# A new program order for all engines of a windowed attention and two mixture layers, with the first key loads in another sequence

## Chip, cores and metric

The kernel runs on one core of a Trainium2 chip. The metric is the device time of one execution in microseconds (us); lower is better. A core has five engines that run their own instruction lists: TensorE (PE, matrix products), VectorE (DVE), ScalarE (ACT), GpSimd (POOL) and SyncE (SP, which here only starts DMA transfers). An engine takes its instructions strictly in the order in which the program lists them, and waits on semaphores for what other engines or transfers must deliver.

## The reference

Three parts, one behind the other; attention has batch 4, 8 heads, 512 local and 32 global tokens and head size 64, d_model is 512.

```python
def _attn_ref(q_l, k_l, v_l, q_g, k_g, v_g):
    k_all = np.concatenate([k_g, k_l], axis=2)
    v_all = np.concatenate([v_g, v_l], axis=2)
    out_g = np.matmul(sm(scale * np.matmul(q_g, k_all.transpose(0, 1, 3, 2))), v_all)
    s_ll = np.where(np.abs(pos[:, None] - pos[None, :]) <= 32, scale * q_l @ k_l^T, -1e9)
    s_lg = scale * np.matmul(q_l, k_g.transpose(0, 1, 3, 2))
    a_l = sm(np.concatenate([s_lg, s_ll], axis=-1))
    return np.concatenate([out_g, np.matmul(a_l, v_all)], axis=2)

def _moe_ref(x, w1, w2, w3, w_out):              # d_ff 768
    return np.maximum(np.maximum(x @ w1, x @ w2), x @ w3) @ w_out

def _moe2_ref(x, w_gate, w_val, w_out):          # d_ff 1536
    return (1.0 / (1.0 + np.exp(-(x @ w_gate))) * (x @ w_val)) @ w_out
```

The output is 2176 x 512 in float32. The weights arrive as 64-bit floats, q, k and v as 32-bit floats.

## The kernel before

**Weights.** The seven weight matrices are read as pairs of 32-bit words and made into float32 on the chip. For w1, w2, w3 and w_out this is `conv_a(i)`, for 24 tiles of 128 x 512: tiles 0 to 17 are w1 to w3 (tile i is matrix i mod 3, block f = i div 3 of 128 columns), tiles 18 to 23 are the six row blocks of w_out. Its steps are: 0, the load of 524 KB by SP (L302 or L305); 1, the low words scaled, on ACT (L285) for even tiles and on DVE (L287) for odd ones; 2, the high words scaled on ACT (L289); 3 and 4, two bit operations on DVE (L291, L294), behind which the tile is a float32 tile; 5, a rounded copy on ACT (L312); 6, the rest by a subtraction on POOL (L271). The raw tiles share memory slots, so that a load waits until the last reader of the slot is done.

**Attention.** It goes by 32 units (batch, half of the sequence, pair of heads). A unit t has the steps `lqk`/`lg` (loads), `pqk` (q and k transposed, on PE at L526 for units 0 to 7, on DVE at L563 to L575 for the others), `sc` (scores on PE, L613, and four fused mask and minimum steps on DVE, L619), `sm` (softmax: ACT L648, DVE L654 and L662, then a copy into a transposing DMA at L697, step 12, or PE transposes at L670), `pv` (v split in parts) and `av` (product with v on PE, L757 or L767; the result scaled on ACT, L783, and its rest on DVE, L785). Every second unit of the second half also has the 32 global tokens: `scg`, `smg` (softmax of these: DVE L709, ACT L715, DVE L718 and L720, then PE transposes at L725) and `avg` (PE L800, DVE L809). The first loads are `lg` of chunk 0: `k0` and `q0` bring heads 0 and 1 (131 KB each; `k0` also brings the small pieces `kx`, 131 KB for all heads), `k1` and `q1` heads 2 to 7 (393 KB each), `v0` and `v2` the v rows; step 0 of `g` brings the global q (66 KB).

**First mixture layer.** Four units make one chunk c (256 tokens, or 288 with the global ones), c = 0 to 7. `l1_c_f_wi` multiplies the chunk by one tile of w1, w2 or w3 and keeps the maximum (DVE L880, L883); `l2_c_m` multiplies the result by w_out for 128 output columns m. Chunk 0 takes whole float32 weights and values (PE L869 for l1, L905 for l2); its l2 has two steps of products, the first with tiles 18 to 22, the second with tile 23, and then a copy by ACT (L912). The products are recorded as two entries of the trace for each tile. The other chunks take rounded pairs, three products each (L321 to L323).

**Second mixture layer.** It multiplies by blocks with seven products in place of eight (L1025, L1212) and writes out through four buffers in `out4` (L1219).

**The order of the work.** Every step of every part is numbered when it is listed (`put`, `once`). One list, `ORDER`, L22 on, holds all 3388 numbers once, and the program is written out in that sequence:

```python
    with tc.manual_schedule():
        for n in order:
            ev[n][2]()
```

Each step puts its instructions at the end of its engines' lists, so `ORDER` sets the sequence on all engines and DMA queues at once, and the waits follow from the data and the buffers. The first loads of k go on ACT's queue for chunk 0, the others on SP's (L424).

## Time and profile before

| | us |
|---|---|
| Runs of the kernel before | 836.99, 837.1, 838.78 |
| Median | 837.1 |
| Profiled execution, its own time | 837.76 |
| Its span, first to last instruction | 836.0 |
| TensorE busy | 809.5 (97%) |
| VectorE busy | 602.7 (72%) |
| ScalarE busy | 477.9 (57%) |
| GpSimd busy | 148.0 (18%) |
| TensorE's mean granted clock | 0.99 |

The profile is of one execution. Its own time is 1.76 us longer than the span of instructions. An engine that is busy 97% leaves some 26 us in which it does nothing, and the tables by stretch tell where these lie.

### The profile page before, as it was taken

Reading aid. Unit: us, or ns where it says so; the run is one execution under the profiler, and the core shown is the slowest. Engines: PE = TensorE matmul, PEld = TensorE weight load, DVE = VectorE, ACT = ScalarE, POOL = GpSimd, SP = SyncE. Lnnn points to the kernel's source line nnn. Section 1 sums busy time; section 2 is a strip of 40 time slices with the busy share of each in tenths; the row PEclk is TensorE's granted clock in tenths of the full one; section 3 lists DMA queues with packets and bytes.
Section 4 is the critical chain, followed back from the end, with each engine's and each line's share of the span. In section 5 each row is a group of like instructions: output and inputs, shape, how many; then the busy total and the mean of one; then the engine's idle time right before and its main releaser. Section 6 shows DMA issues by size and latency. Waiting matters only on the chain.

```text
span 836.0 us, 18171 instructions
## 1 busy us (share of the span) xinstructions
PE 809.5 (97%) x6854; PEld 759.3 (91%) x6854; DVE 602.7 (72%) x1302; ACT 477.9 (57%) x1150; POOL 148.0 (18%) x149
## 2 busy tenths in 40 slices
PE   5899699999999999999999999999999999999997
PEld 3688489898999988999999999999999998999997
DVE  3979857766686667765486978988775669977862
ACT  4987456746565665564446757565645366544441
POOL 3142236333323232423140000000000000000000
PEclk9999799999999999999999999999999999999999
DMA  8977435535553555535443345967342369535311
GB/s 204 279 180 186 97 74 99 104 76 98 102 112 69 90 106 110 103 84 89 144 139 120 126 155 171 314 196 240 120 139 70 126 196 355 192 115 181 114 39 40
DMA packets 217592, 116.09 MB, mean 139 GB/s; under 512 B 161056, under 2 KB 204576, under 8 KB 217504
## 3 DMA queue, kind: packets, MB, share of 16 engines
q1 hardware_dynamic: 214848, 114.27, 50.6%
q8 instruction: 54, 0.88, 0.5%
q10 hardware_dynamic: 2656, 0.66, 0.4%
q14 instruction: 34, 0.28, 0.1%
HBM read 74.91 MB, written 28.57 MB: 124 GB/s over the span
## 4 chain that ended last, share of the span: by engine, by line
PE 88%; DVE 4%; ACT 3%; DMA 2%; issue 1%; SPq 1%; POOL 0%; POOLq 0%; ACTq 0%; DVEq 0%
PE pa L1025 17%; PE ps L321 10%; PE ps L323 9%; PE ps L322 9%; PE pe L1025 8%; PE pa L1212 8%; PE pe L1212 4%; PE pb L1025 4%; PE ps L869 3%; PE sp L613 3%; PE pb L1212 2%; PE ot L767 2%; PE ps L905 2%; PE sg L630 2%; PE acc L1189 1%
## 5 line engine op out<-in xcount | busy, mean ns | idle before, releaser
L1025 PE MATMUL pa<-m,m 128*128 128x384 f32 (+1 forms) x864 | 155.1, 327 | 0.2 <-ACT sn L1031 0.2
L321 PE MATMUL ps<-xt,m 128*128 128x288 f32 (+1 forms) x504 | 149.2, 296 | 1.1 <-DVE h L883 1.0
L323 PE MATMUL ps<-xt,m 128*128 128x288 f32 (+1 forms) x504 | 146.9, 291 | 0.0
L322 PE MATMUL ps<-xt,m 128*128 128x288 f32 (+1 forms) x504 | 145.0, 288 | 0.3 <-DVE xt L858 0.3
L1025 PEld LDWEIGHTS pa<-m,m 128*128 128x128 f32 x864 | 144.5, 188 | 0.8 <-ACT sn L1031 0.7
L321 PEld LDWEIGHTS ps<-xt,m 128*128 128x128 f32 x504 | 94.7, 188 | 9.0 <-issue 4.5
L322 PEld LDWEIGHTS ps<-xt,m 128*128 128x128 f32 x504 | 94.8, 188 | 0.5 <-DVE xt L858 0.5
L323 PEld LDWEIGHTS ps<-xt,m 128*128 128x128 f32 x504 | 94.6, 188 | 0.0
L1031 ACT COPY sn<-pa 128x384 f32<-128x384 f32 (+1 forms) x108 | 49.7, 460 | 61.6 <-PE pa L1025 61.2
L1025 PE MATMUL pe<-m,m 128*128 128x384 f32 (+1 forms) x432 | 83.4, 327 | 0.4 <-ACT m L1194 0.4
L1025 PEld LDWEIGHTS pe<-m,m 128*128 128x128 f32 x432 | 72.8, 188 | 0.9 <-ACT m L1194 0.6
L883 DVE TENSOR_TENSOR h<-ps,h 128x288 f32<-128x288 f32 (+1 forms) x90 | 39.1, 437 | 47.9 <-PE ps L323 38.7
L1212 PE MATMUL pa<-m,m 128*128 128x256 f32 x576 | 72.0, 283 | 0.0
L1212 PEld LDWEIGHTS pa<-m,m 128*128 128x128 f32 x576 | 70.4, 192 | 0.0
L648 ACT ACTIVATE sm<-sm,st 128x224 f32<-128x224 f32 x128 | 60.7, 477 | 10.0 <-DVE st L619 9.7
L1150 ACT CAST m<-m 128x768 fp32r<-128x768 f32 x44 | 36.6, 836 | 44.1 <-PE pa L1212 13.9
L271 POOL TENSOR_TENSOR h<-h,h 128x288 fp32r<-128x288 f32 (+1 forms) x42 | 41.1, 982 | 98.3 <-ACT h L888 94.4
L694 DVE TENSOR_TENSOR pc<-sm,pc 64x512 f16<-64x512 f32 (+1 forms) x72 | 50.5, 701 | 6.5 <-ACT pc L691 5.6
L1155 DVE TENSOR_TENSOR m<-m,m 128x768 fp32r<-128x768 f32 x44 | 41.5, 956 | 17.9 <-ACT m L1150 17.1
L619 DVE CUSTOM_DVE_ANT_0 sm<-sp,mask 128x224 f32<-128x224 f32 x128 | 43.8, 383 | 12.4 <-PE sp L613 9.1
L321 PE MATMUL ps<-h,m 128*128 128x288 f32 (+1 forms) x168 | 50.4, 300 | 0.0
L322 PE MATMUL ps<-h,m 128*128 128x288 f32 (+1 forms) x168 | 48.5, 289 | 0.6 <-POOL h L271 0.6
(192 smaller groups left out, 1651.9 us busy)
## 6 DMA issues: line engine op xcount, KB each, us to landing
m<-in_moe_w_dram SPq DMA_DIRECT2D x18, 512.0 KB, 5.9
gd<-sgt SPq DMA_DIRECT2D x48, 192.0 KB, 2.6
m<-gd SPq DMA_DIRECT2D x6, 1536.0 KB, 8.2
m<-in_moe_w_val_dram SPq DMA_DIRECT2D x6, 1024.0 KB, 5.1
wr<-in_moe_w_out_dram SPq DMA_DIRECT2D x6, 1024.0 KB, 6.2
m<-in_moe_w_gate_dram SPq DMA_DIRECT2D x5, 1024.0 KB, 5.3
vr<-in_v_l_dram SPq DMA_DIRECT2D x48, 96.0 KB, 2.4
x2d<-x2s SPq DMA_DIRECT2D x32, 128.0 KB, 2.0
```

The source lines that it names most:

```text
L271: nc.gpsimd.tensor_tensor(out=out, in0=a, in1=f32(b), op=ALU.subtract)
L321: nc.tensor.matmul(ps, lhsT=wh, rhs=xh, start=first, stop=False)
L322: nc.tensor.matmul(ps, lhsT=wh, rhs=xl, start=False, stop=False)
L323: nc.tensor.matmul(ps, lhsT=wl, rhs=xh, start=False, stop=last)
L619: nc.vector.tensor_tensor_reduce(out=sm[:, hh, j], in0=sp[hh][:, j, 0:224], in1=mask[:, half + j, :], scale=-SC, scalar=3.0e38, op0=ALU.ad ...
L648: nc.scalar.activation(sm4[:, i], sm4[:, i], AF.Exp, bias=st[:, 0, i:i + 1], scale=-1.0, accum_out=st[:, 2, i:i + 1])
L694: nc.vector.tensor_tensor(out=l_, in0=s_, in1=h_, op=ALU.subtract)
L883: nc.vector.tensor_tensor(out=a, in0=ps[:, 0:n], in1=a, op=ALU.max)
L1025: nc.tensor.matmul(ps, lhsT=w[l][:, a, i], rhs=x[m][:, i], start=(k in (1, 2, 5) and i + l + m == 0), stop=(k in (2, 3, 4) and i == 1 and ...
L1031: nc.scalar.copy(t[:, 0:n], pend[u]["a"][:, 0:n])
L1155: tt(out=lo, in0=src[op], in1=f32(hi), op=ALU.subtract)
L1212: nc.tensor.matmul(ps, lhsT=g[l][:, f], rhs=wo_op(b, f, m), start=(k in (1, 2, 5) and f + l + m == 0), stop=(k in (2, 3, 4) and f == 5 and ...
```

## The change

`ORDER` is written anew: the same 3388 numbers, 48 of them at their old place. In the loads of chunk 0's keys only `k0` stays on ACT's queue and `k1` goes on SP's; the pieces of `kn` are loaded ahead of the two of `kx`; behind `k0` a one-column tile is set by VectorE and copied by ScalarE. In `out4` the buffer's index is worked out from t and d. No step is added, left out or changed in what it computes.

```diff
 ORDER = [
-    57, 0, 56, 62, 58, 63, 64, 65, 66, 5, 6, 59, 67, 68, 69, 70, 71, 7, 161, 162, 74, 8, 75, 76, 77, 95, 96, 1861,
...
+    256, 257, 57, 0, 56, 59, 62, 63, 64, 67, 68, 69, 70, 71, 1861, 74, 75, 76, 77, 223, 58, 161, 162, 1862, 1863, 95,
...
+    warm = at.tile([P, 1], F32, name="warm")
...
-        dma = nc.scalar.dma_start if what[0] == "k" and c == 0 else nc.sync.dma_start
+        dma = nc.scalar.dma_start if what == "k0" else nc.sync.dma_start
...
-            if (c, "kn") not in u:
-                kx = slot(("kx", c), (H, D))
-                u[c, "kn"] = slot(("kn", c), (2, H, D)), kx
+            first = (c, "kn") not in u
+            if first:
+                u[c, "kn"] = slot(("kn", c), (2, H, D)), slot(("kx", c), (H, D))
+            kn, kx = u[c, "kn"]
+            for j in range(2):
+                dma(out=kn[:, j, hs], in_=k_l[b, hs, k0 + P * j:k0 + P * j + P, :].rearrange("h s d -> s h d"))
+            if first:
                 dma(out=kx[0:32], in_=k_l[b, :, k0 + HS:k0 + 288, :].rearrange("h s d -> s h d"))
                 dma(out=kx[32:64], in_=k_g[b].rearrange("h s d -> s h d"))
-            for j in range(2):
-                dma(out=u[c, "kn"][0][:, j, hs], in_=k_l[b, hs, k0 + P * j:k0 + P * j + P, :].rearrange("h s d -> s h d"))
+            if what == "k0":
+                nc.vector.memset(warm, 0.0)
+                nc.scalar.copy(warm, warm)
...
-    n_out = [0]
-
     def out4(i, t, d):
         s = pend[i]
-        o = mem(AO + 256 * (n_out[0] % 4), (256,))
-        n_out[0] += 1
+        o = mem(AO + 256 * (2 * t + d), (256,))
```

The positions in `ORDER` of the steps that are spoken of (label, its number, position before, position after; the last figure of a label is the step within its part):

| step | number | before | after | step | number | before | after |
|---|---|---|---|---|---|---|---|
| lg_0_q0 | 57 | 0 | 2 | smg_7_0 | 345 | 454 | 516 |
| lg_0_k0 | 56 | 2 | 4 | smg_7_1 | 346 | 531 | 517 |
| lg_0_q1 | 59 | 11 | 5 | smg_7_3 | 348 | 546 | 532 |
| wa_5_0 | 1861 | 27 | 14 | smg_7_4 | 349 | 547 | 537 |
| lg_0_k1 | 58 | 4 | 20 | smg_7_5 | 350 | 569 | 539 |
| g_0_0 | 5 | 9 | 26 | sc_9_1 to _4 | 405 on | 509 to 520 | 524 to 527 |
| wa_0_0 | 1826 | 35 | 78 | pqk_11_0, _1 | 470, 471 | 510, 511 | 519, 522 |
| lg_0_v0 | 60 | 55 | 101 | l1_0_5_2_1 | 1359 | 523 | 511 |
| wa_18_4 | 1956 | 502 | 367 | sm_8_4, _5 | 379, 380 | 533, 534 | 540, 542 |
| wa_19_4 | 1963 | 549 | 470 | av_7_2 | 344 | 556 | 520 |
| wa_20_4 | 1970 | 558 | 478 | pv_8_2 | 390 | 583 | 531 |
| wa_21_4 | 1977 | 559 | 480 | sm_8_12 | 387 | 644 | 649 |
| wa_22_4 | 1984 | 478 | 485 | lqk_14 | 591 | 678 | 612 |
| wa_23_4 | 1991 | 541 | 501 | lqk_16 | 678 | 654 | 624 |
| l2_0_0_0 | 1362 | 561 | 505 | kg_2 | 30 | 800 | 574 |
| l2_0_3_0 | 1374 | 560 | 507 | wa_12_6 | 1916 | 706 | 659 |
| l2_0_3_1 | 1375 | 565 | 512 | l1_1_4_0_0 | 1410 | 708 | 660 |
| l2_0_2_0 | 1370 | 573 | 518 | sm_2_9 | 149 | 193 | 187 |
| l2_0_1_0 | 1366 | 567 | 535 | wa_3_3, _4 | 1850, 1851 | 195, 196 | 92, 111 |
| l2_0_1_1 | 1367 | 578 | 536 | wa_2_3 | 1843 | 189 | 195 |
| wa_20_0 | 1966 | 471 | 469 | wa_11_1 | 1904 | 199 | 184 |
| wa_22_0 | 1980 | 391 | 464 | sc_5_1 | 237 | 216 | 186 |
| wa_23_0 | 1987 | 481 | 455 | pqk_6_1 | 280 | 175 | 205 |

## Rows read from the trace of the kernel before

**Rows 1.** The page, part 2: TensorE's granted clock in 40 equal slices, tenths.

```profile
PEclk9999799999999999999999999999999999999999
```

**Rows 2.** Busy time by stretch: start:end, its length, then each engine, clock, DMA share, GB/s.

```profile
core 0: us, PE busy (x) PEld busy (x) DVE busy (x) ACT busy (x) POOL busy (x), PEclk, DMA share, GB/s
0.00:9.00 9.00, 2.18 (x7) 1.00 (x7) 0.74 (x2) 2.03 (x5) 6.38 (x26) 1.00 0.69 149
9.00:41.00 32.00, 27.20 (x200) 19.70 (x202) 25.82 (x83) 26.13 (x89) 3.15 (x2) 1.00 1.04 271
41.00:92.00 51.00, 50.93 (x328) 41.26 (x326) 45.12 (x119) 38.74 (x106) 17.41 (x14) 0.97 0.74 180
92.00:107.00 15.00, 7.83 (x19) 5.92 (x20) 9.61 (x18) 5.62 (x20) 3.05 (x3) 0.66 0.18 40
...
110.00:450.00 340.00, 337.71 (x3729) 310.82 (x3729) 234.27 (x638) 195.72 (x565) 118.05 (x105) 1.00 0.48 99
450.00:831.00 381.00, 380.42 (x2563) 377.78 (x2561) 286.71 (x444) 208.65 (x365) 0.00 (x0) 1.00 0.49 164
```

**Rows 3.** Timeline of the start, PE and ACT: start, us, engine, line, operation, [idle before].

```profile
5.59 1.28 ACT L551 ACT_TABLE_LOAD   x1 [5.59 <-DMA m<-in_k_l_dram]
8.26 0.60 ACT L551 COPY kw<-tk 128x64 f32<-128x64 f32 x3 [1.39 <-PE tk L526]
...
13.27 0.77 PE L526 MATMUL tk<-ident,m 128*128 128x128 f32 x2 [1.67 <-DMA m<-in_k_l_dram]
...
28.80 1.10 PE L757 MATMUL ot<-pw,m 96*64 96x128 f32 x16
```

**Rows 4.** Timeline of 83 to 108 us, all engines, in order of time.

```profile
83.75 2.19 SPq L305 DMA_DIRECT2D m<-in_moe_w_out_dram  x2
...
91.29 0.71 PE L905 MATMUL ps<-hw,m 128*128 128x256 f32 x2
...
97.53 1.49 POOL L271 TENSOR_TENSOR m<-m,m 128x512 fp32r<-128x512 f32 x1 [3.89 <-DMA vrw<-in_v_l_dram]
...
97.92 1.22 PE L905 MATMUL ps<-hw,m 128*128 128x256 f32 x2 [5.92 <-DVE m L294]
98.12 1.45 DVE L291 SCALAR_TENSOR_TENSOR m<-m 128x512 int32<-128x512 int32 x1
99.60 1.30 DVE L294 SCALAR_TENSOR_TENSOR m<-m 128x512 int32<-128x512 int32 x2
...
100.39 9.16 PE L905 MATMUL ps<-hw,m 128*128 128x256 f32 x28 [1.25 <-issue]
...
107.44 0.37 ACT L912 COPY x2s<-ps 128x256 f32<-128x256 f32 x1 [9.75 <-PE ps L905]
```

**Rows 5.** Timeline of PE: the first group of l1, chunk 0 and chunk 1.

```profile
41.29 2.02 PE L869 MATMUL ps<-xw,m 128*128 128x256 f32 x4
...
117.51 0.40 PE L321 MATMUL ps<-xt,m 128*128 128x288 f32 x1
```

**Rows 6.** The chain that ended last, a piece of it behind 110 us.

```profile
110.11 3.03 PE ps L905 x14
```

**Rows 7.** Groups of DVE's instructions, 80 to 101 us: busy us, mean ns, idle before.

```profile
L294 DVE SCALAR_TENSOR_TENSOR m<-m 128x512 int32<-128x512 int32 x7 | 4.8, 693 | 0.1
L619 DVE CUSTOM_DVE_ANT_0 sm<-sp,mask 128x224 f32<-128x224 f32 x7 | 2.4, 380 | 0.0
...
L662 DVE TENSOR_TENSOR sm<-sm,st 128x896 f32<-128x896 f32 x1 | 1.1, 1092 | 0.0
...
L709 DVE TENSOR_REDUCE stg<-sgs 128x1 f32<-128x640 f32 x1 | 0.8, 805 | 0.0
...
L720 DVE TENSOR_SCALAR eg<-eg,stg 128x640 f32<-128x640 f32 x1 | 0.6, 553 | 0.1
...
L711 DVE TENSOR_SCALAR stg<-stg 128x1 f32<-128x1 f32 x1 | 0.1, 141 | 0.0
```

**Rows 8.** Waits of SP's DMA queue: waited for, us in total, times, longest.

```profile
SPq L487 <- POOL vb L591: 15.3, 10, 2.7
```

337 rows, old and new, of the table ORDER are left out of this document.

## The prediction, made before the changed kernel was run

> **What bounds the kernel now.** I read the page first: TensorE's granted clock falls below 0.9 in one slice of 20.9 us, the fifth [rows 1]. The busy table by stretch says where TensorE's time goes [rows 2]: of 0 to 9 us it works 2.18, of 9 to 41 it works 27.20, of 92 to 107 it works 7.83. From 41 to 92 it misses 0.07, from 110 to 450 2.29 of 340 and from 450 to 831 0.58 of 381; the last 5 us are the end of the output. So an order of steps can win something at the start and between 92 and 107, and nearly nothing elsewhere.
>
> At the start [rows 3] TensorE transposes keys (L526) and waits for loads of k, 1.67 at 13.27, which is the first use of heads 2 to 7, for unit 3. ScalarE's one table load lies at 5.59 to 6.87, and ScalarE then waits 1.39 for TensorE's result.
>
> The stretch 92 to 107 is the first chunk's w_out product, l2 (L905) [rows 4]. Its first pair of records ends at 92.00; the next pair starts at 97.92 after 5.92 of waiting for VectorE's last conversion step of w_out tile 19 (L294), and the one after that waits 1.25 more; tiles 20 and 21 are finished by 99.60 + 1.30 = 100.9. The copy of the finished group starts at 107.44, so its last product ended about 107.24. From 91.29 to 107.24 TensorE ran 22 records (2, 2 and 18 of the 28). One costs 3.03/14 = 0.216 at the full clock [rows 6], so 22 are worth 4.76 us: 15.95 - 4.76 = **11.2 us lost**. 7.17 of these are the two waits. The other 4.0 are the clock: 0.66 over 15 us [rows 2] is (1 - 0.66) x 15 = 5.1 us missing, so some 10.2 us of that stretch at the lower of the two levels, 1.2 instead of 2.4 GHz, right behind the 5.92 us of waiting.
>
> **The change, part by part.** *l2 of chunk 0.* VectorE had no idle time to speak of from 80 to 101 (0.0 or 0.1 ahead of each group [rows 7]), so what counts is what stands in its list ahead of the last w_out conversion. By the table of positions, fourteen VectorE steps that stood ahead of it now stand behind tile 23's, and nothing new stands ahead. By form [rows 7]: smg_7_0 0.81 (L709), the four mask steps of sc_9 4 x 0.38 = 1.52 (L619), sm_8_5 1.09 (L662); the other eight steps (pqk_11_0 and _1, l1_0_5_2_1, sm_8_4, smg_7_1, _3 and _4, av_7_2) have ten instructions from smg_7_4's 0.55 (L720) to smg_7_1's 0.14 (L711), 3.1 together. Sum 6.5. So the last conversion ends at 100.9 - 6.5 = 94.4, and tile 22's, with tile 23's L291 and L294 behind it (0.7 each), at 93.0 at the latest. TensorE now runs l2_0_0_0 and l2_0_3_0 (tiles 18 to 22) and only then l2_0_3_1 (tile 23). Starting at 91.29 it reaches the fifth tile after 8 records, at 93.0, and tile 23 after 20, at 95.6. So the waits of 7.2 shrink to between nothing and 1 us, and with a TensorE that comes 1.5 earlier (below) while VectorE does not, to 1.5 or so. I take 1.5 and no lower clock, as no wait near 5.92 is left before it: regained 11.2 - 1.5 = **9.7**. The upper bound is 11.2. The lower one: the loads of w_out tiles 20 to 23 need raw slots that GpSimd frees; the longest wait of a load for GpSimd's L591 in the trace is 2.7 [rows 8], and if the clock falls all the same its 5.1 stay: 11.2 - 2.7 - 5.1 = 3.4.
>
> What covers the fourteen steps: TensorE needs their results only behind l2. The nearest is unit 7's global softmax, whose smg_7_4 must be done before its transposes (L725, smg_7_5). Of the fourteen all but sm_8_4 and sm_8_5 stand ahead of its end, and pv_8_2 (a cast, 0.4): 94.4 + 6.5 - 1.25 + 0.4 = 100.1. TensorE comes to L725 behind 44 records of l2, at 91.29 + 44 x 0.216 = 100.8, or 99.3 with the start's gain. So the cover is 0.7, or 0.8 short; I count that in the 1.5 above, and behind it each us late costs one.
>
> These conversions have a second price. One L291 step took 1.45 at 98.12 while GpSimd's subtraction of 97.53 to 99.02 (L271) ran [rows 4]; the seven L294 steps of the same shape took 0.69 on the mean [rows 7]: 0.76 for the meeting. That meeting is in the 100.9 already; two new ones add 1.5, inside the bounds. The Trainium skill (SBUF — State Buffer, section "Who interferes with whom") states that a VectorE instruction with two SBUF inputs contends with a GpSimd instruction that reads SBUF, and that the loser blocks for the whole instruction. The 1.45 of L291 agrees; by that rule no reorder that moves GpSimd steps next to conversions is free, and two new meetings would take the 9.7 down to 8.2.
>
> *First key loads.* k1 (393 KB) goes from ScalarE's queue to SP's, as the fourth load there (behind q0, q1, wa_5), and wa_0 (524 KB) and the first g load (66 KB), which were in flight before k1 was complete, come later. By size, q0 131, k0 131 + 131, q1 393, wa_5 524, k1 393 make 1.70 MB up to k1, against 2.29 MB before. At 149 GB/s up to 9 us (1.34 MB) and 271 behind [rows 2] the new k1 is there at 9 + 0.36/0.271 = 10.3; the same sum gives 12.5 for before, where the row shows 13.2. So unit 3's keys come 2.2 to 2.9 earlier, 2.6. On the way to the first l1 group (41.29 [rows 5]) the new list puts more VectorE work ahead of unit 2's last softmax step (sm_2_9): wa_3_3 and wa_3_4 in and wa_2_3 out (one step of 0.69 net [rows 7]), sc_5_1 in (0.38), wa_11_1 in for pqk_6_1 (two short ones, alike): 1.1. 2.6 - 1.1 = **1.5**. Bounds 0 (VectorE, 25.82 of 32 busy, decides) and 2.9. Against it: v0 now lies behind 1 MB more of weights, 3.7 us at 271 GB/s; I cost that at nothing, as the first product with v (L757) was at 28.80 [rows 3], behind scores and softmax of its unit; without that cover it costs what is over.
>
> The Trainium skill (DMA: Bandwidth & Descriptors, section "Issuing engines are not separate DMA queues") says that starting DMAs on several engines saves the issuing time alone, since all of them share the same 16 DMA engines. By that rule the move of k1 to SP's queue wins nothing in itself, and the start's 1.5 would be 0; the sequence of bytes is what I count.
>
> *kn before kx, the early activation, out4.* Scores of unit 0 need all four k0 pieces, so their sequence changes nothing (0 to 0.5). The table load lies 5.59 to 6.87 and ScalarE then waits 1.39 for TensorE [rows 3], which waits for k: moved earlier, it hides as before; the memset and the one-column copy are of the size of L711's 0.14 [rows 7], on engines idle there. out4 takes the same four buffers in the same rotation: nothing.
>
> *Behind 107 us.* The list is new everywhere, but TensorE's sequence differs only locally there, and it misses 2.3 + 0.6 = 2.9 in 721 us [rows 2]: no more than that can come back. What can be lost lies in l1 of chunk 1, which comes 11 us earlier with the work around it unchanged. VectorE is busy 234.27 of the 340 from 110 on, 69%, and was 45.12 of 51, 88%, from 41 to 92, where TensorE missed 0.07 [rows 2]: it has room. But some tiles of w1 to w3 are converted just ahead of their use: GpSimd's step wa_12_6 stands directly ahead of l1_1_4_0 in the new list (659, 660). I take +1.0, with two such steps of 1.49 (L271 [rows 4]), 3.0, as the upper bound and -2.9 as the lower.
>
> Sum: -1.5 - 9.7 + 1.0 = -10.2 on the profiled execution, which took 837.76: 827.6. The median of the runs shown is 0.66 below that, so **826.9**. About 0.2% (1.7 us) is what a measurement of this kernel can tell from no change.
>
> **The rivals.** *A: the start gives nothing.* All loads share one stream of bytes, whatever queue k1 is on, and VectorE decides, not the keys; for it 25.82 of 32 busy, against it the 1.67 wait at 13.27. 837.1 - 8.7 = 828.4.
> *B: the conversions are still late.* Loads held by GpSimd's slots, new port meetings, a clock that falls: l2 gives 3.4 only. 837.1 - 1.5 - 3.4 + 1.0 = 833.2. For it the two loads of 83.75, which took 2.19 to issue [rows 4]; against it that the loads of tiles 20, 22 and 23 stand earlier in the new list.
> *C, slower: SP's queue.* The transposing loads (L697) now stand behind loads that wait for a buffer: sm_8_12 behind lqk_14, lqk_16 and kg_2, by the positions. Loads waited for GpSimd's buffer ten times, 15.3 us together [rows 8]; once such a wait is longer than the work between a transpose and its product on TensorE, it passes through. All ten passed through: 837.1 - 10.2 + 15.3 = 842.2. Against it: GpSimd is busy 118.05 of 340 us there, and TensorE missed 2.3 of them although the ten waits were there [rows 2].
> *D: it doesn't do what it says.* The chain of unit 7's global softmax takes the place of the conversions and the l1 of chunk 1 comes at 117.51 again [rows 5]; the start's gain is waited away there too: 836.9. For it that this chain has no cover; against it that it is 0.8 short by the sum above, where 9.7 would be needed.
>
> **Chances.** Forecast 0.70, A 0.10, B 0.10, C 0.06, D 0.04. The range goes from 822 (start 2.9, l2 11.2, and half the waits behind 110, 1.4, make 15.5: 821.6) to 834, which takes in A and B; D and C stay out. Faster 0.90, same 0.04 (D), slower 0.06 (C).
>
> **What would show it.** The first l1 group at 39 to 40 instead of 41.29; unit 3's key transposes at 10.3 to 11.0; no wait over 2 us at L905 and a clock near 1.0 where it was 0.66; the first L321 of chunk 1, 117.51 before, at 105 to 108; the end as far behind it as before, within 1 us. Wrong, if TensorE still waits at L905 for L294, if the clock still falls there, or if waits of over 2 us appear behind 110.

## The result, and the profile after

The changed kernel took 841.3 us in the median of twelve runs (838.0 to 846.1), the kernel before 836.6 in twelve beside them (834.3 to 839.7): 1.0063 times as long [1.0039, 1.0086], so slower by 0.6%. Its profiled execution took 839.93 with a span of 838.2, 2.2 more than the span before.

The busy table by stretch of the changed kernel, columns as in [rows 2]:

```profile
9.00:41.00 32.00, 29.66 (x206) 22.01 (x205) 28.17 (x86) 27.14 (x98) 1.30 (x1) 1.00 1.09 264
41.00:92.00 51.00, 47.07 (x321) 38.85 (x320) 48.54 (x105) 38.94 (x103) 19.90 (x14) 1.00 0.70 178
92.00:107.00 15.00, 13.93 (x102) 11.59 (x102) 13.38 (x35) 7.02 (x19) 7.42 (x7) 1.00 0.34 65
...
450.00:831.00 381.00, 372.00 (x2486) 366.37 (x2485) 280.58 (x441) 201.07 (x358) 0.00 (x0) 1.00 0.49 161
```

Against [rows 2] two stretches are better and two are worse. From 92 to 107 TensorE works 13.93 instead of 7.83, at a granted clock of 1.00 instead of 0.66, and from 9 to 41 it works 29.66 instead of 27.20. But from 41 to 92 it now misses 3.93 (it missed 0.07), and from 450 to 831 it misses 9.00 (it missed 0.58). In the last stretch VectorE and ScalarE are less busy than before, not more: the steps there are the same, they only take longer.

The timeline of the changed kernel, PE (start, us, engine, line, operation, [idle before]). Its line 876 is line 869 of before, 912 is 905, 322 is 321, 1032 is 1025, 1038 is 1031:

```profile
10.48 0.93 PE L533 MATMUL tk<-ident,m 128*128 128x128 f32 x3
...
13.94 1.87 PE L620 MATMUL sp<-kw,qw 64*128 64x224 f32 x8 [1.01 <-ACT kw L558]
...
38.03 4.16 PE L876 MATMUL ps<-xw,m 128*128 128x256 f32 x18
...
54.25 1.64 PE L620 MATMUL sp<-kw,qw 64*128 64x224 f32 x8 [1.17 <-DVE st L626]
...
74.66 1.97 PE L876 MATMUL ps<-xw,m 128*128 128x256 f32 x8 [0.78 <-issue]
77.81 2.00 PE L876 MATMUL ps<-xw,m 128*128 128x256 f32 x8 [1.18 <-DVE h L890]
...
86.96 2.00 PE L876 MATMUL ps<-xw,m 128*128 128x256 f32 x8 [0.40 <-DVE m L295]
...
91.31 1.57 PE L912 MATMUL ps<-hw,m 128*128 128x256 f32 x6
93.24 0.71 PE L912 MATMUL ps<-hw,m 128*128 128x256 f32 x2 [0.36 <-DVE m L295]
94.62 8.02 PE L912 MATMUL ps<-hw,m 128*128 128x256 f32 x36 [0.67 <-issue]
...
107.36 0.40 PE L322 MATMUL ps<-xt,m 128*128 128x288 f32 x1
...
432.31 0.40 PE L322 MATMUL ps<-h,m 128*128 128x288 f32 x1 [0.17 <-DVE h L890]
```

The first l1 group starts at 38.03 instead of 41.29 [rows 5], 3.3 earlier. The first l2 product, however, starts at 91.31, exactly where it started before (91.29, [rows 4]): the 3.3 are waited away on the way, at 54.25, 74.66, 77.81 and 86.96 (1.17 + 0.78 + 1.18 + 0.40 = 3.5; three of the four for VectorE, the second with no releaser in the profile). Then l2 runs almost through, with waits of 0.36 and 0.67, and the first l1 product of chunk 1 comes at 107.36 instead of 117.51 [rows 5], 10.15 earlier. What was won is there, and it is all of it in front of 108 us.

Behind it the lead melts. I read the start of the first l2 product of chunk 7 off both timelines; that of the kernel before:

```profile
440.20 0.29 PE L321 MATMUL ps<-h,m 128*128 128x288 f32 x1
```

From chunk 1's first l1 to there it took 322.7 before and 324.95 after, 2.3 more; from there to the end of the span 395.8 before (836.0 - 440.2) and 405.9 after (838.2 - 432.3), 10.1 more. The account closes: 0.0 at 91.3, -10.2 for l2, +2.3, +10.1, together +2.2.

Most of the 10.1 are waits in the second mixture layer. Two terms help to read them. A weight block of that layer is made by the steps `w_prep`: a load, conversions, sums, then parts rounded by ScalarE (L995, L1005) and the rests that VectorE subtracts (L1009 to L1014). A bank is the accumulator in which TensorE sums up a product; before the next product can go on in it, ScalarE copies it (L1038), or VectorE sums it out (L1051). The waits of TensorE, 432 to 836 us of the changed kernel (waited for, us in total, times, longest):

```profile
PE pa L1032 <- ACT sn L1038: 2.3, 2, 1.2
PE pb L1032 <- DVE m L1009: 1.3, 1, 1.3
PE pa L1032 <- ACT m L995: 1.2, 2, 0.6
PE pa L1032 <- DVE m L1009: 1.2, 2, 0.9
PE pa L1032 <- DVE m L994: 0.8, 1, 0.8
PE pa L1032 <- DVE m L972: 0.7, 1, 0.7
PE pe L1032 <- DVE sgt L1051: 0.7, 1, 0.7
PE pa L1219 <- ACT sn L1224: 0.5, 1, 0.5
PE pa L1032 <- ACT m L1201: 0.4, 1, 0.4
...
```

They sum to 9.1. The kernel before has two waits in that layer:

```profile
PE pe L1025 <- ACT m L1194: 0.4, 1, 0.4
PE pa L1025 <- ACT sn L1031: 0.2, 1, 0.2
```

So the waits make 8.5 of the 10.1. TensorE is also busy 3.3 longer from there to the end, 393.2 against 389.9, for practically as many products (a product right behind a wait takes longer: the six records at 512.58 take 1.34, undisturbed ones of that size 1.20), and the tail behind its last product is 1.5 shorter. No row is large and no releaser stands out. Sorted by what is waited for: 4.5 for a weight block being prepared (L994, L995 and L1009, steps of `w_prep`), 3.5 for a bank that is copied or summed out (L1038, L1224, L1051), 1.1 for others. Two places show how such a wait comes about.

The timeline of the changed kernel around 512 and 634 us, ScalarE, VectorE and TensorE:

```profile
510.02 1.16 ACT L286 ACTIVATE wr<-wr 128x1024 uint32<-128x1024 uint32 x1 [1.70 <-DMA wr<-in_moe_w_out_dram]
...
512.04 0.86 ACT L1038 COPY sn<-pa 128x384 f32<-128x384 f32 x2
512.58 0.62 PE L1032 MATMUL pa<-m,m 128*128 128x384 f32 x2 [1.15 <-ACT sn L1038]
...
633.99 1.15 ACT L1005 CAST m<-m 128x512 fp32r<-128x512 f32 x2
635.17 0.69 DVE L1009 TENSOR_TENSOR m<-m,m 128x512 fp32r<-128x512 f32 x1 [5.84 <-ACT m L1005]
635.92 0.97 PE L1032 MATMUL pb<-m,m 128*128 128x384 f32 x4 [1.32 <-DVE m L1009]
```

In the first, ScalarE's next instruction is a conversion (L286) that waits 1.70 for its load, then takes 1.16, and a second one of 1.11 follows; the copy of the bank that TensorE wants back stands behind them in ScalarE's list, and TensorE waits 1.15. In the second, the weight block itself is late: VectorE's subtraction L1009 starts when ScalarE's casts (L1005) are done, VectorE has sat idle for 5.84 before it, and TensorE waits 1.32 for its result. VectorE is idle for 5.84 right before it makes TensorE late, in a stretch in which it is busy 280.58 of 381, 74%.

In the kernel before most blocks are ready well ahead. Its timeline, the last preparing step of a block (L1007) and the stretch of products that begins with the block's first:

```profile
585.90 1.23 DVE L1007 TENSOR_TENSOR m<-m,m 128x1024 fp32r<-128x1024 f32 x1
...
594.11 2.10 PE L1025 MATMUL pa<-m,m 128*128 128x320 f32 x12
```

The step ends at 587.1; the block's first product, by its place in the list the second half of this row, starts at 595.0. For the same kind of block in the changed kernel:

```profile
589.89 1.39 PE L1032 MATMUL pa<-m,m 128*128 128x320 f32 x8
...
593.15 1.22 DVE L1014 TENSOR_TENSOR m<-m,m 128x1024 fp32r<-128x1024 f32 x1
```

Here the block's first product starts at 590.8, within the first row, and the last preparing step ends at 594.4, 3.6 later (the first products need only the parts that are finished). Of the twelve blocks seven had a margin of 7 to 8 us before, the others between -1.5 and 20; in the new list one has 9.3, two have next to nothing (0.2 and 0.0), and nine are late by 0.5 to 5.1. A second margin shrank in part: between two products on the same bank, with ScalarE's copy between them, stood two other products in 105 of 108 places of the old list; in the new list it is a single one in 32 of 108, two in 25, and three or more in 51.

### The profile page after: what moved, and what is told of

Its sections match the earlier page's. It is cut to its first block, busy times and chain, and to the rows that moved or that the text cites. A ratio compares the mean times of both kernels' runs of the same rounds, so it can differ in the third digit from the quotient of the medians.

```text
span 838.2 us, 18095 instructions
## 1 busy us (share of the span) xinstructions
PE 803.0 (96%) x6854; PEld 758.0 (90%) x6854; DVE 615.6 (73%) x1303; ACT 473.9 (57%) x1151; POOL 153.0 (18%) x149
## 5 line engine op out<-in xcount | busy, mean ns | idle before, releaser
L1032 PE MATMUL pa<-m,m 128*128 128x384 f32 (+1 forms) x864 | 158.0, 328 | 6.5 <-ACT sn L1038 2.3
L1038 ACT COPY sn<-pa 128x384 f32<-128x384 f32 (+1 forms) x108 | 49.2, 463 | 86.6 <-PE pa L1032 82.5
L1032 PE MATMUL pe<-m,m 128*128 128x384 f32 (+1 forms) x432 | 81.4, 327 | 0.7 <-DVE sgt L1051 0.7
L272 POOL TENSOR_TENSOR h<-h,h 128x288 fp32r<-128x288 f32 (+1 forms) x42 | 39.4, 942 | 101.2 <-ACT h L895 83.1
L701 DVE TENSOR_TENSOR pc<-sm,pc 64x512 f16<-64x512 f32 (+1 forms) x72 | 55.4, 770 | 2.7 <-ACT pc L698 1.6
```

The source lines that it names most:

```text
L272: nc.gpsimd.tensor_tensor(out=out, in0=a, in1=f32(b), op=ALU.subtract)
L701: nc.vector.tensor_tensor(out=l_, in0=s_, in1=h_, op=ALU.subtract)
L1032: nc.tensor.matmul(ps, lhsT=w[l][:, a, i], rhs=x[m][:, i], start=(k in (1, 2, 5) and i + l + m == 0), stop=(k in (2, 3, 4) and i == 1 and ...
L1038: nc.scalar.copy(t[:, 0:n], pend[u]["a"][:, 0:n])
```

## The experiments

The list was taken apart first. In the diffs the numbers of `ORDER` are steps, and the lists are cut down to a few steps around the first places that change. The kernels have the new key loads and the early activation, but for three: the second experiment's, and the two that start from the kernel before (the fourteen steps and the four conversions). Ratios are to the kernel before, run beside each on the same chip.

**The loads alone.** Old list, new `at_load_group`, `out4` and activation:

```diff
 ORDER = [
-    256, 257, 57, 0, 56, 59, 62, 63, 64, 67, 68,
+    57, 0, 56, 62, 58, 63, 64, 65, 66, 5, 6, 59,
...
```

> The list of before with the new first loads and the early activation alone. Theory 1: the profile of the kernel with the old list up to the second layer shows the same front: first l1 group at 38.95 instead of 41.29, l1 of chunk 1 at 119.06 instead of 117.51; so 837 to 839, no gain. My prediction's start term (1.5 us won): 834 to 835.5.

836.0 us, 0.9994 [0.9981, 1.0007]: nothing. The first l1 group came at 40.06, 1.2 earlier, and chunk 1 at 118.91, later than the 117.51 of [rows 5]. The Trainium skill (DMA: Bandwidth & Descriptors, section "Issuing engines are not separate DMA queues") says that loads started from several engines share the same DMA engines, so that another issuer by itself saves only issuing time; this run agrees, with 0.9994.

**The list alone**, with the old loads:

```diff
-        dma = nc.scalar.dma_start if what == "k0" else nc.sync.dma_start
+        dma = nc.scalar.dma_start if what[0] == "k" and c == 0 else nc.sync.dma_start
...
```

> The whole new list with the loads of before (k1 on ScalarE's queue, small pieces first, no early activation). Theory 1 and 2: as the changed kernel within 2 us, 839 to 843, since the 3 us won at the first l1 group are gone again by the first l2 group (91.3 in both profiles). Theory 3: 834 to 837, faster than the changed kernel.

853.3 us, 1.0219 [1.0186, 1.0251], 12.0 above the whole change. The timeline of this kernel, ScalarE with its queue's issue, and TensorE:

```profile
14.22 1.04 ACTq L441 DMA_DIRECT2D m<-in_k_l_dram  x2
...
19.42 0.45 PE L527 MATMUL tk<-ident,m 128*128 128x128 f32 x1 [7.18 <-DMA m<-in_k_l_dram]
```

In the new list `lg_0_k1` stands behind unit 0's softmax. On ScalarE's queue it is therefore issued at 14.22, when that softmax is done, and TensorE waits 7.18 for its keys; chunk 0's first l1 slips to 50.67. On SP's queue, where the whole change puts it, it stands behind no computing. So the loads and the list are one edit: the first is worth nothing alone, and the second needs it.

**Where the list wins and where it loses.** New list up to the first l1 product of chunk 1 (576 steps), from there the remaining steps in the old sequence:

```diff
 ORDER = [
...
-    30, 383, 1386, 1387, 1915, 384,
+    30, 383, 164, 165, 131, 132, 119, 235,
...
```

> The new list up to the first group of l1 of chunk 1 (576 steps), behind it all other steps in the sequence of the list before; the new loads. Theory 1 (the gain of the start and of l2 is real, the new sequence behind it gives it back): about 10 us below the kernel before, 826 to 828, TensorE's idle time behind 110 us under 4 us. Theory 2 (whatever is gained ahead is waited away behind, because loads and VectorE set the end): 835 to 838. Theory 3 (the new loads cost something late): above 838.

829.25 us, 0.9921 [0.9905, 0.9937]: the fastest of these kernels, 1.4% ahead of the whole change. Chunk 1 starts at 107.71, and the second layer takes what it took: the busy table of this kernel, two stretches of that layer, and of the whole change for the same two:

```profile
450.00:550.00 100.00, 100.00 (x606) 99.48 (x604) 83.25 (x141) 65.83 (x120) 0.00 (x0) 1.00 0.58 192
550.00:650.00 100.00, 100.00 (x607) 100.00 (x607) 73.19 (x133) 52.77 (x100) 0.00 (x0) 1.00 0.45 155
```

```profile
450.00:550.00 100.00, 97.51 (x584) 95.98 (x583) 77.66 (x134) 61.21 (x112) 0.00 (x0) 1.00 0.56 188
550.00:650.00 100.00, 95.46 (x569) 93.69 (x568) 69.71 (x127) 53.48 (x103) 0.00 (x0) 1.00 0.42 137
```

Both kernels reach the first l2 of chunk 7 at 432.31. The 9.3 by which their spans differ (838.2 and 828.9) lie behind it. So the 2.3 lost ahead of it are hardly the new sequence's own: with the old sequence behind chunk 1 that stretch takes 324.6, 1.9 more than before. What the new sequence does change there cancels: TensorE waits 8.4 in it, where the first cut has 3.3 and the kernel before 1.7, but works 316.4 for practically the same products, where they need 321.3 and 321.0.

The cut at the end of the attention (1913 steps of the new list, then the old one):

```diff
 ORDER = [
...
-    1742, 1743, 1147, 1754, 902, 1994, 1744, 1778,
+    1742, 1743, 1147, 1754, 902, 1750, 1994, 2954, 2897, 1778,
...
```

> The new list up to the end of attention (the first 1913 steps), behind it the sequence of the list before. Theory 1 with the second mixture layer as the place (from 450 us on the lead of 8 us turns into 3 us of lag in the profile): 828 to 831, and the waits at TensorE's products of that layer under 1 us in sum. Theory 2: 836 to 842, with waits of 6 us or more in that layer although its sequence is that of before.

831.7 us, 0.9951 [0.9937, 0.9965]. Between this kernel and the whole change only the steps behind the attention differ, the second layer and the last 81 steps of the first (chunks 6 and 7): 841.3 - 831.7 = 9.6 us. Between it and the first cut lies the rest of the attention: 831.7 - 829.25 = 2.5 by the medians. No profile shows these 2.5 (this kernel's own ran at a lower clock, see the end), so they are not shown to be the sequence's.

The mirror image, old list up to the end of the attention and then the new one:

```diff
 ORDER = [
...
-    1741, 1742, 1312, 1313, 1994, 2954, 2897, 1778, 1743, 1744,
+    1741, 1742, 1312, 1313, 1743, 1754, 1994, 1744,
...
```

> The list of before up to the end of attention (1912 steps), behind it the sequence of the new list; the new loads. Theory 1: the second layer's new sequence costs its 8 to 11 us by itself, 844 to 848. Theory 2: the lag comes only where TensorE arrives early, so here 836 to 838.

848.8 us, 1.0142 [1.0121, 1.0163]: 12.5 above the kernel before. In its profile 8.4 of this lie behind chunk 7's first l2. The loss of the second layer needs nothing of the new front.

A cut in between, new list up to chunk 4's first l1 (1273 steps):

```diff
 ORDER = [
...
-    749, 821, 920, 1594, 1564, 1104,
+    749, 821, 920, 1337, 439, 547, 684,
...
```

> The new list up to the first group of l1 of chunk 4, the old one behind. The profiles have the changed kernel at -8.4 us against before at that point, the kernel with the cut at chunk 1 at -7.3. If the sequence of the attention between these points costs nothing: 828 to 829.5. If the 2.5 us between the two earlier cuts (829.25 and 831.7) are lost here: 830.5 to 832.

833.3 us, 0.9971 [0.9951, 0.9990], 4.0 above the cut at chunk 1. At neither later cut does the new list win anything behind chunk 1, and the three cuts do not stand in the order of their length (829.25, 833.3, 831.7).

**What wins the ten microseconds of l2.** The kernel before, with only the fourteen VectorE steps of the prediction, and what hangs on them, put behind the last conversion step of w_out (in this list tile 21's):

```diff
 ORDER = [
...
-    370, 371, 323, 345, 330,
+    370, 371, 323, 330,
...
-    375, 376, 405, 470, 471,
+    375, 376,
...
```

> The kernel before with its own loads, in which only the fourteen VectorE steps of the prediction (and the steps that hang on them) are moved behind the last conversion of w_out. My step for l2: 6.5 us earlier conversions, no clock fall, 9.7 us won: 826 to 829. If ScalarE's steps (L289) or the loads hold the conversions, 832 to 835; if the moved steps are late next, 836 or more.

834.4 us, 0.9984 [0.9969, 0.9999], and chunk 1's first l1 at 116.12, 1.4 earlier. The timeline of this kernel, VectorE and TensorE:

```profile
92.28 1.01 DVE L288 TENSOR_SCALAR m<-m 128x512 int32<-128x512 uint32 x1 [1.60 <-DMA m<-in_moe_w_out_dram]
94.79 0.69 DVE L292 SCALAR_TENSOR_TENSOR m<-m 128x512 int32<-128x512 int32 x1 [1.50 <-ACT m L290]
...
97.90 1.22 PE L906 MATMUL ps<-hw,m 128*128 128x256 f32 x2 [5.07 <-DVE m L295]
```

With the other work gone, VectorE simply waits: 1.60 for the load of tile 23, whose first step stands next, and 1.50 for ScalarE's part of it. The last steps of tiles 19, 20 and 21, whose loads landed earlier (the last of them, tile 20's, at 89.06, tile 23's at 92.18), stand behind tile 23 in the list, though TensorE wants them first. It still waits 5.07.

So the next kernel moves no other work at all: the kernel before, four conversion steps among themselves (step 4 of tile 19, steps 3 and 4 of tile 20, step 4 of tile 21), ahead of tile 23's first conversion:

```diff
 ORDER = [
...
-    1961, 1962, 1982,
+    1961, 1962, 1963, 1982,
...
-    389, 1976, 411,
+    389, 1976, 1977, 1969, 1970, 411,
...
-    343, 1963, 413,
+    343, 413,
...
-    344, 1969, 1970, 1977, 1374,
+    344, 1374,
...
```

> The kernel before with its own loads and list, in which four VectorE steps alone are moved: the last conversion step of tile 19 directly behind its first, and those of tiles 21 and 20 (three steps) ahead of tile 23's first step, whose load lands last. If the order of the conversions among themselves is what held l2: TensorE's 5.9 us of waiting shrink to 2 to 3 (tile 20 is ready at about 94.7), no clock fall, l1 of chunk 1 at 109 to 111 instead of 117.5, 828 to 831 in all. If VectorE's load of other steps or the loads held it, as my prediction had it: 834 to 836.

832.2 us, 0.9952 [0.9934, 0.9969]. The timeline of this kernel, TensorE:

```profile
96.22 7.75 PE L906 MATMUL ps<-hw,m 128*128 128x256 f32 x28 [3.94 <-ACT sgs L639]
...
111.93 0.40 PE L322 MATMUL ps<-xt,m 128*128 128x288 f32 x1
```

Chunk 1 starts at 111.93, 5.6 earlier, where the fourteen steps gave 1.4 (by the medians 4.3 and 1.4). One wait is left in l2, 3.94 at 96.22; it ends when VectorE is done with tile 20, at 96.12, though the profile names another releaser. The clock from 92 to 107 is 0.89. The sequence of the conversions among themselves is thus the larger part of the 10.2, and the fourteen steps alone are 1.4; what of the new front makes the rest was not separated.

Whether the earlier loads of tiles 20 and 23 are a part of it, was tried on the first cut, with the issuing steps `wa_23_0` (1987) and `wa_20_0` set back:

```diff
 ORDER = [
...
-    404, 306, 1987, 1975, 1976, 401, 275, 276, 332, 333,
+    404, 306, 1975, 401, 275, 332, 1980, 1981, 1962, 315, 118, 468, 1987, 1976, 276, 333,
...
```

> The kernel of the new list up to l1 of chunk 1 and the old behind (829.25), in which the loads of w_out tiles 23 and 20 stand behind the load of unit 11's q and k on SP's queue, so that they are issued near 84 us as before and not at 75.3 and 81.1. If early loads are what won at l2: TensorE waits 3 to 6 us at L912 again, the clock falls there, 833 to 838. If VectorE's list won it: 829 to 830.5.

829.5 us, 0.9917 [0.9901, 0.9933], as without this edit. The test settles little: tile 23's load was issued only 4 us later and landed at 83.3, still ahead of its use, and tile 20's was not later at all (issued at 80.0, in the first cut at 80.8). So whether the earlier loads are a part of the gain stays open; tile 20's landed at 87.73 in the kernel before and, as the last of the six, at 84.7 in the changed one.

**What the second layer loses by.** Two margins had shrunk, the weight blocks' and the spacing on a bank. First the blocks: the new list, with the weight preparation (`w_prep` and the second product's weights) back where the old list has it, counted in products that lie ahead:

```diff
 ORDER = [
...
-    2973, 2974, 2975, 1997, 1815,
+    2973, 2974, 2975, 2967, 2968, 1997, 1815,
...
```

> The new list, but the steps that load and convert the weights of the second layer (w7 and wo, 234 steps) stand where the list before has them, counted in products of that layer that lie ahead of them: 8 to 9 products (16 to 18 us) earlier on the mean than in the new list; all else keeps the new sequence. Theory 1a (these steps, moved close to their use, are what gives the gain back): 831 to 835, near the run with the whole second layer in the old sequence (831.7). Theory 1b (the new sequence of the products themselves or of the outputs gives it back): 839 to 843, as the changed kernel.

857.6 us, 1.0274 [1.0238, 1.0310], 16 worse than the list it should mend. (This expectation put a product at 2 us; the 252 products take 250.9 us of TensorE in the kernel before, 1.0 each.) The waits of TensorE in the second layer of this kernel:

```profile
PE pa L1032 <- ACT sn L1038: 6.8, 9, 1.1
PE pe L1032 <- DVE sgt L1051: 6.3, 4, 2.3
PE pb L1032 <- DVE sgt L1051: 3.3, 1, 3.3
PE pa L1032 <- ACT sgt L1054: 2.2, 1, 2.2
PE pe L1032 <- DVE tm L1051: 1.1, 1, 1.1
PE pa L1219 <- ACT sn L1224: 0.5, 1, 0.5
```

No wait for a weight block is left, where the new list has 4.5; the waits for banks have grown from 3.5 to 20.2 (in a profiled execution of 864.4). The preparation is ready in time again, and stands ahead of the copies instead.

The reverse on the first cut, weight preparation as late as in the new list:

```diff
 ORDER = [
...
-    2966, 1769, 1794, 2967, 2968, 2969, 1796,
+    2966, 1769, 1794, 2969, 1796,
...
```

> The reverse: the kernel of the new list up to l1 of chunk 1 and the old behind (829.25), with the steps w7 and wo alone moved as late as the new list has them (9 products later on the mean). Theory 1a: 836 to 841, most of the 9.6 us between the changed kernel and the one with the old second layer. Theory 1b: 828 to 831, no change.

850.5 us, 1.0168 [1.0151, 1.0185], 21 us above the first cut, and more than the whole change loses. Products moved along with the steps they need (71 of the 252 stand at another place of their sequence), so this is not the margin alone.

Finer versions of it, on the first cut: the closing steps (9 to 13) of the weight blocks late, and all steps of the blocks late, without the second product's weights. Products moved along here too, 28 and 97 of them, and left a single product between two on a bank in 12 and 25 places, where the first cut has 2:

```diff
 ORDER = [
...
-    3011, 2047, 3029, 3136, 3012, 3013, 2048, 2489,
+    3011, 2047, 3029, 2489,
...
```

> The kernel of the new list up to l1 of chunk 1 and the old behind (829.25), in which the last steps of each weight block of the second layer (w7, steps 9 to 13, VectorE's and ScalarE's closing steps; 43 of them) stand as few products ahead of the block's first product as in the new list: the last one 0 to 5 products ahead or just behind it, not 10 or 11. Theory 1a (cover of 7 to 8 us in the old list, none in the new one): 832 to 838, TensorE waiting for VectorE's L1009 and L1012. If the cover was not needed: 829 to 830.

```diff
 ORDER = [
...
-    1813, 1996, 1999, 3014, 2000, 2394, 2001,
+    1813, 1996, 1999, 2000, 2394, 2001,
...
```

> The same for all steps of w7 (loads and conversions too, 129 steps), each directly ahead of the next product, so that they stand behind ScalarE's copies of the product before and not ahead of them as in the earlier run at 850. Theory 1a: 836 to 842. If the 850 came from the conversions standing ahead of the copies (TensorE waited 11.6 us for L1038), TensorE's waits for L1038 fall below 4 us here; if it came from the lateness alone, it is 848 to 852 again.

855.4 us, 1.0236 [1.0211, 1.0262], and 852.3 us, 1.0207 [1.0182, 1.0233]. In both the largest wait is again for the bank's copy, L1038, 13.0 us in eight and 11.0 in eleven places, not for the blocks.

The spacing: the first cut, with the second layer's products, copies and outputs in the new sequence and everything else in the old:

```diff
 ORDER = [
...
-    2983, 1825, 1998, 2393, 1813, 1996, 1999,
+    2983, 1825, 2393, 1998, 1813, 1996, 1999,
...
```

> The same base (829.25), in which the products of the second layer, their copies and their outputs stand among themselves as in the new list, while the preparation of the weights keeps a gap of 4 to 7 products on the mean. Theory 1a (the gap): 829 to 833. Theory 1b (the new sequence of the products): 836 to 841, with waits at L1038's copies.

845.2 us, 1.0100 [1.0084, 1.0116], 16 above the first cut; L1038 is waited for 5.9 us in four places. This is not the spacing alone: with the products moved, the last closing step of eleven of the twelve blocks stands at most 6 products ahead of the block's first, where the old list has 9 to 11 for eight of them. And the new list with the blocks' own steps at the old margin:

```diff
 ORDER = [
...
-    2409, 2935, 2009,
+    2409, 2935, 2984, 2009,
...
```

> The whole new list, in which the weight preparation w7 alone stands as many products ahead of its block's first product as in the old list (10 instead of 0 on the mean), each step directly ahead of a product and behind the copies. Theory 1a: 831 to 835. Theory 1b: 838 to 842.

870.2 us, 1.0420 [1.0395, 1.0445], the slowest of all. L1038 is waited for 11.5 us, against 2.3 in the new list.

So two smaller ones. On the first cut, one product in 24 units set one place earlier, so that a single product is left between two on a bank; nothing else moves:

```diff
 ORDER = [
...
-    2080, 2561, 2081, 2553, 3045, 2554, 2082, 3158,
+    2080, 2561, 2082, 2081, 2553, 3045, 2554, 3158,
...
```

> The kernel of the new list up to l1 of chunk 1 and the old behind (829.25), in which in 24 units of the second layer the product 6 stands directly behind 5, ahead of the product 4 of the unit before: one product of TensorE (about 1 us) instead of two between product 1 and product 6, which waits for ScalarE's copy of the bank (0.46 us). Theory 1b (the distance covers the copy when it stands behind a conversion of 1.1 to 1.2 us on ScalarE): 832 to 838, with waits at L1038's copies of 3 us or more. If the distance does not matter: 829 to 830.

831.2 us, 0.9945 [0.9925, 0.9966]: 2.0 above the first cut, with overlapping intervals, and the three waits on L1038 together are 1.3. The short spacing by itself costs some 2 us by the medians, and anything from nothing to 4 within the intervals. And the new list with that spacing repaired, 8 places of one product instead of 32, other products moved by two at most:

```diff
 ORDER = [
...
-    1812, 1999, 2394, 2000, 2001, 2980,
+    1812, 2000, 1999, 2394, 2980,
...
```

> The whole new list, in which those places of the second layer that have one product between are given two where the data allow it (32 places become 8; all other steps move by two products at most). Theory 1b: 835 to 839, waits at L1038 under 1 us. If the distance does not matter: 840 to 842.

851.0 us, 1.0200 [1.0160, 1.0239], ten above the new list; the waits for weight blocks grew from 4.5 to 7.2 (L995 3.9, L1009 2.0 and 1.3). A shift of two products is more than the new list has to spare.

Last the margin with all products in place: the first cut, the closing steps of six blocks two products ahead of the first use, with the loads of the next blocks, which need the buffers that these steps read, behind them:

```diff
 ORDER = [
...
-    2067, 2527, 3022, 3023, 3148, 2068, 3024, 2069,
+    2067, 2527, 3022, 3148, 2068, 2069,
...
```

> The same base as the first (829.25), all products in place, in which the closing steps (9 to 13) of six weight blocks stand two products ahead of the block's first product instead of 9 to 11, with the next load of that buffer behind them. Theory 1a (the gap): 832 to 836, TensorE waiting for L1009 or L1012 at the first products of those blocks, up to 1 us each. If a gap of two products is enough: 829 to 830.

866.8 us, 1.0377 [1.0355, 1.0399]. The timeline of this kernel, ScalarE and TensorE:

```profile
608.00 1.10 ACT L286 ACTIVATE m<-m 128x1024 uint32<-128x1024 uint32 x1 [6.37 <-DMA m<-in_moe_w_val_dram]
...
610.35 0.41 ACT L1038 COPY sn<-pa 128x320 f32<-128x320 f32 x1
...
610.81 2.61 PE L1032 MATMUL pa<-m,m 128*128 128x320 f32 x8 [5.29 <-ACT sn L1038]
```

The clearest case of the mechanism, though not of the margin: the load came late, ScalarE stood 6.37 at the conversion that wants it, and TensorE waited 5.29 for the copy of 0.41 that stands behind. Nine waits on L1038 make 26.4 us in this kernel, and ScalarE's five waits at L286 for loads of `w_gate` and `w_val` 29.2. TensorE's trace names the copy; the cause is the load in the first row.

The clock adds to such waits. The busy table of this kernel, from 550 to 650 us:

```profile
550.00:650.00 100.00, 82.29 (x447) 80.32 (x446) 59.36 (x107) 42.35 (x79) 0.00 (x0) 0.90 0.40 138
```

The granted clock is 0.90, where the first cut and the whole change have 1.00: from 553 to 559 it is 0.50, the lower of TensorE's two levels, where TensorE waited 4.01 up to 554.59, and it falls again at four later waits of 3.8 to 5.3. By an estimate from that row up to (1 - 0.90) x 100 = 10 us of work are lost so, beside the waiting. The late closing steps (0.91 in that stretch) and the early blocks' steps (0.93) show the same; the late blocks' steps (0.98) and the products alone (1.00) hardly do. So the times of some of these exchanges hold more than the waits that they bring.

## Why the prediction was wrong

Forecast were 826.9 us, 822 to 834, and a faster kernel; measured were 841.3 and a slower one.

**The start, -1.5: mis-sized, and it did not last.** Unit 3's keys came as worked out: their transposes start at 10.48, inside "10.3 to 11.0", and its scores at 13.94, where they started at 16.51 before, 2.6 earlier, the number of the prediction. The table load at 2.95 is hidden, as forecast. The first l1 group gained more than the bound of 2.9 allowed (3.3). But nothing of it arrived at the first l2, 91.31 to 91.29. (One pair of profiles tells this to a microsecond or two: the two kernels that start from the kernel before reach the first l1 at 43.99 and 42.90 with the same front, and the first l2 at 92.1 and 91.1; kernels with the new front and a full clock from 9 to 41 us reach l2 between 89.7 and 91.3.) The prediction said why it could fail: TensorE comes earlier "while VectorE does not". It put the 1.5 of waiting into l2; it was 3.5, and it fell in l1, where VectorE is busy 48.54 of 51. For the kernel as a whole the start gave what rival A said, nothing, though not because the bytes came no sooner.

**l2 of chunk 0, -9.7: the right size, by luck, for a reason half right.** From the first l2 to chunk 1's first l1 it took 26.22 before and 16.05 after, 10.2 less; the waits at L912 are 0.36 and 0.67 (together 1.0, taken as 1.5), and the clock stayed at 1.00. The step "fourteen VectorE steps that stood ahead of it now stand behind tile 23's" is true of the list and was priced at 6.5 of VectorE's time (the last conversion ended at 95.9, where 94.4 was worked out); done alone it gave 1.4, so that the term came out at its size is luck. The prediction did not ask in what sequence the conversions stand to each other. Tile 19 is needed second and stood behind tile 23, whose load landed at 91.31; four steps moved among themselves gave 5.6. The low clock was a consequence of the waiting, as read: with the waits gone it was 1.00.

**Behind 107 us, +1.0 with bounds -2.9 and +3.0: the step that failed.** Measured +12.3 in the profiles, 2.3 before chunk 7's l2 and 10.1 behind it. Of the first part 1.9 appear with the old sequence too, once the front is early; of the second hardly any (0.7 at the first cut). By the medians the cuts put 9.6 on the steps behind the attention. The text said that "TensorE's sequence differs only locally there" and that VectorE at 69% "has room". In the second layer 200 of 252 products stand at another place of the sequence of products. And the busy share bounds nothing here: the 9.1 us of waits arose while VectorE was busy 280.58 of 381 us and ScalarE 201.07. An engine that takes its list in turn can have a quarter of its time to spare and still be late at single hand-overs. The rows that would have told were to be had: the distance between the last step of a weight block and its first product (7 to 8 us before in seven of twelve) and the spacing on a bank can be read from the trace of before and the two lists, hand-over by hand-over, without the new trace. The prediction did this for the 15 us of l2 and let two averages stand for the 721 behind it. The bound of +3.0, "two such steps of 1.49", took late preparing steps of GpSimd in l1 of chunk 1, and two of them; in the second layer, where GpSimd is busy 0.00, there were twelve waits, for VectorE and ScalarE.

**The rivals.** C had the sign, slower, by another mechanism: of waits on a transposing load one is left, 1.16 at 248.84. B and D fell: l2 gained in full, and unit 7's transposes (L732) started at 102.47, 6.9 earlier. No rival had the second layer in it. One reading in B is wrong by the table of positions: the load of tile 22 stands later in the new list (391 to 464), not earlier; only those of 20 and 23 stand earlier.

**The markers.** Right: unit 3's keys, no wait over 2 us at L912, the clock near 1.0, chunk 1 at 107.36 within "105 to 108". Wrong: the first l1 at 38.03 instead of 39 to 40, and "the end as far behind it as before, within 1 us", which was off by 12.3. The sign named for it, waits over 2 us behind 110, would hardly have shown it: one of 2.18 in the attention, and none over 1.4 in the layer that lost most.

**What is settled and what is open.** Shown: the new list wins some 10 us ahead of chunk 1, of which 7.0 reach the end if the old sequence follows (829.25 against 836.2), and loses about 9.6 behind the attention, by cuts in both directions. Shown too: that loss is, for 8.5 of the 10.1 in the profile, waiting at hand-overs in the lists of ScalarE and VectorE, half of it for weight blocks and nearly two fifths for banks, and the one exchange in the new list that took away the first kind (4.5 to 0) brought more of the second (3.5 to 20.2). Open: which single property of the new list makes the 9.6. The spacing on the banks alone makes some 2. Every other exchange of a group of steps of that layer gave a kernel slower than both whole lists, by 4 to 29 us against the new one, and in part by a lower clock, so none of them can be read as the price of its group. The margin of the weight blocks alone was not isolated, since the loads behind it moved too. Open as well: what the medians of the cuts inside the attention (833.3 and 831.7 against 829.25) owe to the sequence and what to the clock.

## What to carry to other kernels

Before you price a new order of steps by an engine's busy share, take the hand-overs one at a time: for each result that the bounding engine needs, how long ahead of its use does the last step end, and what stands in front of that step in its engine's list, above all an instruction that waits for a load. A list from a search is worth cutting: run its front with the old rest and its rest with the old front; here the front alone was 0.8% faster than before and the whole 0.6% slower. Exchanges of one group of steps between the two lists told less: they brought waits of their own. And an edit of the list and an edit of who issues a load can need each other, as a load is issued in its engine's turn.

## What was not expected of the hardware

The same front ran at two clocks. The busy table of the cut at the end of the attention, in its profiled execution, which took 837.8 us where the median is 831.7:

```profile
9.00:41.00 32.00, 29.66 (x184) 21.74 (x184) 24.25 (x77) 23.72 (x82) 1.30 (x1) 0.84 1.09 264
```

TensorE is as busy as in the changed kernel (29.66) and does 184 instructions instead of 206, at a granted clock of 0.84, a mean of its two levels, instead of 1.00; the first l1 group starts at 42.12 instead of 38.03 and chunk 1 at 113.15 instead of 107.36, so 5.8 us later, with the same steps in the same sequence. In both, two waits of TensorE, of 0.85 and 0.5, stand at 21.7 and 22.9; behind them the clock fell in the one (0.50 from 24 to 28 us) and stayed in the other. Two more of the kernels with the new front had such a profile. Over the changed kernel's twelve runs the mean clock of the span goes from 0.988 to 1.000, and the profiled one has 1.000: that may be in part why the median stands 1.4 above the profile. What sets the one or the other was not tried.
